# The last batch's output product as seven block products for eight, with the block sums on GpSimd and VectorE

## The chip, the cores and the metric

One core of one Trainium2 chip. The metric is the device time of one execution in microseconds (us). A time is the median of several executions. Times were taken in rounds against the kernel before on the same chip; all runs quoted are in the normal ("fast") state of the chip.

## The reference

Two attentions, then a small two-layer network. B = 8 batches, H = 8 heads, S = 576 positions, D = 64; the network has 512 inputs, 2048 hidden units and 512 outputs.

```python
def _attn_ref(q, k, v, p):
    scale = 1.0 / np.sqrt(q.shape[-1])
    # sm_attn(q, k, v) = softmax(scale * q k^T) v
    p_packed = sm_attn(p, k, v)          # 32 rows per head
    return sm_attn(q, p_packed, p_packed)

def _moe_ref(x, w_in, w_out):            # x: (4608, 512), heads side by side
    h = x @ w_in
    g = h * np.cos(h)
    return g @ w_out
```

## The kernel before

TensorE is the busy engine. Batch by batch, `h_mm` makes the hidden units of a batch in 16 pieces of 128 (TensorE into PSUM, ScalarE a sine, VectorE the product `gT`), and the output product of the *previous* batch is spread between these as filler matmuls. The last batch has no successor, so its output product stands alone at the end.

Each batch has 576 rows: four chunks of 128, and 64 left over. Two batches' leftovers make one "joint" chunk, copied together by GpSimd.

```python
    def h_mm(b, fc):
        ...
        def rest():
            V.tensor_tensor(out=gT[b][:, fc, :]..., in0=ps[:, :, 0:HS], in1=csv, op=ALU.mult)
            if fc % 8 == 7:
                j0 = (b % 2) * 64
                G.tensor_copy(out=joint[b // 2][:, fc - 7:fc + 1, j0:j0 + 64],
                              in_=gT[b][:, fc - 7:fc + 1, 512:576])
        return rest
    ...
    def tail_chunk(b, c):                       # the joint chunk of the last pair of batches
        osb = o_pool.tile([128, DM], FP32, name="osb")
        for i in range(2):
            cols = slice(i * 256, i * 256 + 256)
            ps = O.tile([128, 256], FP32, name="ot", tag="ot")
            for fc in range(NFC):
                nc.tensor.matmul(ps, joint[b // 2][:, fc, :], w_out_bf[:, fc, cols], ...)
            copy((ACT, V)[i], osb[:, cols], ps)
            for (a, z, rows), q in zip(pieces_of(b, c), (nc.sync, nc.scalar)):
                q.dma_start(out=rows[:, cols], in_=osb[a:z, cols])
    ...
    # the end of the kernel
    out_eng[:] = V, ACT
    set_filler(B - 1)      # drains batch 6, then chunks 0 to 3 of batch 7: 64 matmuls of 512 columns
    fill(1000)
    tail_chunk(B - 1, 4)   # 32 matmuls of 256 columns
```

PSUM is split into a pool `A` of three double banks (for `h_mm` and all else) and a pool `O` of two single banks (output chunks).

## Time and profile before

| | |
|---|---|
| median time | 248.45 us (3 runs), 248.26 with one more |
| span of the profiled execution | 246.8 us |
| TensorE busy | 94% |
| last stretch, from the seven leftover filler matmuls on (223.84) to the last copy's end (243.33) | 19.49 us |
| from there to the end of the span ("store tail") | 3.42 us |

The views give a span to 0.1 us; the ends of spans, and so the store tails, are taken here and below from the trace files, in ns (this span is 246.753 us). The prediction's 3.47 us for the tail comes from the rounded 246.8.

The prediction below shows the lines. They are read like this: a line of the time order has the start in us, the length in us, the engine, the source line, what was written from what, shapes, and a count; in brackets the engine's idle time before it and what ended that. The chain of waits lists, in order of time, what each piece of the path to the end consisted of.

### The profile page before, as it was taken

What the parts mean: (1) busy time and instruction counts of PE and PEld (TensorE: products, weight loads), DVE (VectorE), ACT (ScalarE), POOL (GpSimd) and SP (SyncE); (2) the same over time, 40 slices, a digit from 0 to 9 for tenths busy, and PEclk for the clock granted to TensorE, in tenths of its full rate; (3) what the DMA queues carried; (4) which work ended last, traced back from release to release, by engine and by line L of the source; (5) the groups of instructions that cost most, each with busy time, mean ns of one, the idle gap of its engine ahead of it and who ended that gap; (6) DMA issues with size and microseconds to landing.
All of it is one profiled execution on the core that took longest, in us unless ns stands there. A gap on an engine that the chain in (4) does not pass through costs nothing.

```text
span 246.8 us, 5023 instructions
## 1 busy us (share of the span) xinstructions
PE 233.2 (94%) x1996; PEld 130.9 (53%) x2029; DVE 165.2 (67%) x248; ACT 169.0 (68%) x282; POOL 57.7 (23%) x70
## 2 busy tenths in 40 slices
PE   8788799999999999999999999999999999999993
PEld 3454374566545654565446554565456554665452
DVE  3549987677658776678767766678766684886110
ACT  2369799877576787888787776888778684873000
POOL 8342533240400355004503105030500100001000
PEclk9999999999999999999999999999999999999999
DMA  6999999999899999999999997999571113111133
GB/s 90 202 203 206 205 206 228 194 241 151 179 202 184 192 175 214 218 198 142 222 211 187 172 201 91 198 166 171 109 154 27 45 43 84 43 31 57 47 84 85
DMA packets 64231, 37.36 MB, mean 151 GB/s; under 512 B 36848, under 2 KB 59632, under 8 KB 64208
## 3 DMA queue, kind: packets, MB, share of 16 engines
q0 software_dynamic: 23152, 18.75, 50.0%
q1 hardware_dynamic: 40624, 18.09, 35.1%
q8 instruction: 16, 0.26, 0.4%
q10 hardware_dynamic: 432, 0.20, 0.4%
q14 instruction: 7, 0.06, 0.1%
HBM read 37.22 MB, written 9.44 MB: 189 GB/s over the span
## 4 chain that ended last, share of the span: by engine, by line
PE 78%; DMA 12%; issue 2%; DVE 2%; ACT 2%; POOL 2%; DVEq 0%; POOLq 0%
PE ot L309 46%; PE psA L256 21%; DMA vbf<-in_v_dram 10%; PE psA L207 3%; DMA a1T<-a 2%; PE psA L129 2%; PE psA L183 2%; DVE gT L263 2%; PE ot L295 1%; PE psA L233 1%; ACT cosT L260 1%; POOL vp L77 1%; ACT ppT L75 1%; POOL kbf L84 1%; PE ot L104 0%
## 5 line engine op out<-in xcount | busy, mean ns | idle before, releaser
L309 PE MATMUL ot<-w_out_bf,gT 128*128 128x512 bf16 x482 | 127.5, 379 | 2.0 <-issue 1.1
L263 DVE TENSOR_TENSOR gT<-psA,cosT 128x576 bf16<-128x576 f32 x128 | 93.8, 755 | 28.9 <-ACT cosT L260 28.2
L260 ACT ACTIVATE cosT<-psA 128x576 bf16<-128x576 f32 x128 | 82.4, 652 | 24.6 <-PE psA L256 22.1
L256 PE MATMUL psA<-a2n,PPW 128*128 128x288 bf16 x512 | 83.8, 286 | 1.6 <-DVE gT L263 0.4
L309 PEld LDWEIGHTS <-gT 128*128 128x128 bf16 x512 | 47.8, 98 | 43.4 <-issue 6.7
L256 PEld LDWEIGHTS <-PPW 128*128 128x128 bf16 x512 | 49.3, 98 | 34.6 <-issue 3.9
L77 DVE CAST PPW<-psA 128x1024 bf16<-128x1024 f32 (+1 forms) x23 | 26.9, 1175 | 11.6 <-PE psA L207 11.5
L267 POOL COPY joint<-gT 128x512 bf16<-128x512 bf16 x16 | 9.9, 616 | 82.5 <-DVE gT L263 82.5
L77 DVE COPY osb<-ot 128x512 f32<-128x512 f32 (+1 forms) x22 | 14.9, 678 | 17.5 <-PE ot L309 7.7
L77 POOL COPY vp<-vbf 96x3072 bf16<-96x3072 bf16 x7 | 19.3, 2751 | 6.3 <-DMA vbf<-in_v_dram 6.3
L75 ACT COPY osb<-ot 128x512 f32<-128x512 f32 (+1 forms) x15 | 8.5, 567 | 15.3 <-PE ot L309 10.6
L243 DVE SCALAR_TENSOR_TENSOR a2n<-a2u,r,lns 128x576 bf16<-128x576 bf16 x16 | 12.3, 812 | 7.3 <-ACT lns L241 7.3
L235 ACT ACTIVATE lns<-psA 128x576 f32<-128x576 f32 x16 | 10.1, 650 | 7.1 <-PE psA L233 6.5
L140 ACT ACTIVATE a<-psA 128x576 bf16<-128x576 f32 x16 | 10.3, 647 | 6.7 <-PE psA L129 6.7
L309 PE MATMUL ot<-w_out_bf,joint 128*128 128x512 bf16 x47 | 12.8, 379 | 0.1
L225 ACT ACTIVATE a2u<-psA,rs 128x576 bf16<-128x576 f32 x16 | 11.0, 737 | 1.4 <-PE psA L129 1.3
L75 ACT CAST ppT<-psA 64x128 bf16<-64x128 f32 x24 | 6.2, 260 | 7.0 <-DVE ppT L77 5.9
L207 PE MATMUL psA<-w_in_bf,ppT 64*32 64x512 bf16 x224 | 10.1, 380 | 0.0
L241 ACT ACTIVATE lns<-lns 128x576 f32<-128x576 f32 x16 | 10.0, 676 | 0.0
L347 PE MATMUL ot<-wz 128*128 128x512 bf16 x23 | 7.7, 468 | 1.4 <-DVE wz L358 1.2
L527 POOL COPY gate<-kT 1x1 bf16<-1x1 bf16 x3 | 0.5, 181 | 32.3 <-DMA kT<-kbf 32.3
L183 PEld LDWEIGHTS <-vp 96*128 96x128 bf16 x192 | 6.5, 98 | 2.3 <-issue 1.2
(73 smaller groups left out, 152.7 us busy)
## 6 DMA issues: line engine op xcount, KB each, us to landing
kbf<-in_k_dram POOLq DMA_DIRECT2D x8, 576.0 KB, 12.6
vbf<-in_v_dram POOLq DMA_DIRECT2D x8, 576.0 KB, 7.6
qbf<-in_q_dram POOLq DMA_DIRECT2D x8, 576.0 KB, 10.1
out_dram<-osb SPq DMA_DIRECT2D x24, 192.0 KB, 2.7
out_dram<-osb SPq DMA_DIRECT2D x22, 128.0 KB, 2.4
w_in_bf<-in_moe_w_in_dram POOLq DMA_DIRECT2D x4, 512.0 KB, 17.3
w_out_bf<-in_moe_w_out_dram POOLq DMA_DIRECT2D x4, 512.0 KB, 21.2
out_dram<-osb SPq DMA_DIRECT2D x26, 64.0 KB, 2.1
```

The costliest lines, as they stand in the source:

```text
L75: ACT.copy(out=out, in_=in_)
L77: eng.tensor_copy(out=out, in_=in_)
L140: ACT.activation(out=a1[b % 2][:, y, :, 0:TP].rearrange("p (e m) x -> p e m x", e=2), in_=ps[y][:, :, 0:HS].rearrange("p e (m x) -> p e m ...
L183: nc.tensor.matmul(ps[:, hp * 64:(hp + 1) * 64], vp[b][:, c, hp * 128:(hp + 1) * 128], a1T[b][0:TP, :, j, 32 * hp:32 * hp + 32], start=(j ...
L207: nc.tensor.matmul(ps[y][32 * x:32 * x + 32, :], ppT[b % 2][r, 2 * x + y, :], w_in_bf[r, x, n * 512:(n + 1) * 512], start=True, stop=True)
L225: ACT.activation(out=a2u[b][:, y].rearrange("p (e x) -> p e x", e=2), in_=ps[y][:, :, 0:HS], func=AF.Exp, scale=rs1[b][:, y:y + 1])
L235: ACT.activation(out=lns[b][:, y].rearrange("p (e x) -> p e x", e=2), in_=ps[:, :, 0:HS], func=AF.Ln)
L243: V.scalar_tensor_tensor(out=a2n[b][:, y], in0=a2u[b][:, y], scalar=r1[b][:, y:y + 1], in1=lns[b][:, y], op0=ALU.mult, op1=ALU.mult)
L256: nc.tensor.matmul(ps[:, e, 0:HS], PPW[b][:, y, fc * 128:(fc + 1) * 128], a2n[b][:, y, e * HS:(e + 1) * HS], start=(y == 0), stop=(y == 1))
L260: ACT.activation(out=csv, in_=ps[:, :, 0:HS], func=AF.Sin, bias=PI_HALF)
L263: V.tensor_tensor(out=gT[b][:, fc, :].rearrange("p (e x) -> p e x", e=2), in0=ps[:, :, 0:HS], in1=csv, op=ALU.mult)
L309: nc.tensor.matmul(pss[c], w, w_out_bf[:, fc, :], start=(fc == 0), stop=(fc == NFC - 1))
```

## The change

The intent: in the last batch the output product of each pair of chunks (256 rows) is a 2 x 2 block product. Winograd's form of Strassen's algorithm makes it from seven block products, not eight, at the price of sums of blocks. Sums of weight blocks (`T`) go to GpSimd during batch 6, behind a one-element copy that waits for batch 6's normalised probabilities (the gate). Sums of activation blocks (`S`) go half to GpSimd, as the first eight pieces of batch 7 become ready, half to VectorE at the end. The joint chunk moves to the second place, as 16 matmuls of 512 columns. VectorE adds the products up as they leave PSUM.

```diff
+    def T_sums():
+        G.tensor_copy(out=gate, in_=a2n[B - 2][0:1, 1, 0:1])
+        ...
+        for out, in0, in1 in ((T[0], B_blk(0, 1), B_blk(0, 0)), (T[1], B_blk(1, 1), T[0]),
+                              (T[2], B_blk(1, 1), B_blk(0, 1)), (T[3], B_blk(1, 0), T[1])):
+            G.tensor_tensor(out=out, in0=in0, in1=in1, op=ALU.subtract)
+
+    def S_sums(b, p, eng, k0, k1):
+        ...
+        for out, in0, in1, op in ((S1, A21, A22, ALU.add), (S2, S1, A11, ALU.subtract),
+                                  (S3, A11, A21, ALU.subtract), (S4, A12, S2, ALU.subtract)):
+            eng.tensor_tensor(out=out, in0=in0, in1=in1, op=op)
+
+    def last_out(b):
+        ... # o1, o2, u: where the sums of products gather; store: the output DMAs
+            m = {1: (A_blk(b, 2 * p, 0, 0, 8), B_blk(0, 0)), 2: (A_blk(b, 2 * p, 1, 0, 8), B_blk(1, 0)),
+                 3: (S4, B_blk(1, 1)), 4: (A_blk(b, 2 * p + 1, 1, 0, 8), T[3]),
+                 5: (S1, T[0]), 6: (S2, T[1]), 7: (S3, T[2])}
+            def then4(ps, p=p, o1=o1, o2=o2, u=u):
+                plus(o2, ps, u[:, 1])
+                store(o2, 2 * p + 1)
+                plus(o1[:, 2], ps[:, 1], o1[:, 2])
+            def then3(ps, p=p, o1=o1):
+                plus(o1[:, 1], ps, o1[:, 2])
+                store(o1, 2 * p, 1, (nc.sync, nc.scalar, nc.sync))
+        ...
+        def products(names):
+            ps = O.tile([128, 2, 256], FP32, name="ot", tag="ot")
+            for i, (p, n) in enumerate(names):
+                lhs, rhs = pr[p][0][n]
+                for kp in range(8):
+                    nc.tensor.matmul(ps[:, i], lhs[:, kp, :], rhs[:, kp, :], start=kp == 0, stop=kp == 7)
+            ... # then the addition of each
+        products(((0, 1),))
+        ... # the joint chunk: 16 matmuls of 512 columns, ACT.copy, store
+        for names in (((0, 2), (0, 6)), ((0, 7),), ((0, 4), (0, 5)), ((0, 3), (1, 1)),
+                      ((1, 2), (1, 6)), ((1, 7),), ((1, 4), (1, 5)), ((1, 3),)):
+            products(names)
@@ slot: after pieces 3 and 7 of batch 7, GpSimd's share of the S sums
+            if s == B - 1 and fc in (3, 7):
+                for p in range(2):
+                    S_sums(s, p, G, fc // 2 - 1, fc // 2 + 1)
@@ the end
-    out_eng[:] = V, ACT
-    set_filler(B - 1)
     fill(1000)
-    tail_chunk(B - 1, 4)
+    for p in range(2):
+        S_sums(B - 1, p, V, 4, 8)
+    last_out(B - 1)
```

(Cut: tile allocations, the renaming of S to SQ, helper functions.)

> **What bounds the kernel now.** I read the page's busy shares and slices first, then the chain of waits, then the time order of the last 25 us engine by engine, and last the groups of instructions of that stretch. The page and the end of the chain:
>
> ```profile
> PE 233.2 (94%) x1996; PEld 130.9 (53%) x2029; DVE 165.2 (67%) x248; ACT 169.0 (68%) x282; POOL 57.7 (23%) x70
> ...
> PE   8788799999999999999999999999999999999993
> DVE  3549987677658776678767766678766684886110
> POOL 8342533240400355004503105030500100001000
> ...
> 224.00 4.32 PE ot L309 x20
> 228.32 0.05 issue
> 228.37 10.74 PE ot L309 x49
> 239.11 0.05 issue
> 239.16 3.67 PE ot L295 x32
> ```
>
> The reader is to see a TensorE busy to the end, with every other engine nearly idle in the last four slices (24.7 us). The chain's last 19 us are TensorE alone: the output product of the last batch. Whatever shortens that stretch shortens the kernel, unless another engine comes onto the path. The time order of that stretch:
>
> ```profile
> 223.84 15.27 PE L309 MATMUL ot<-w_out_bf,gT 128*128 128x512 bf16 x69
> 239.16 3.66 PE L295 MATMUL ot<-w_out_bf,joint 128*128 128x256 bf16 x32
> ...
> 224.02 1.47 DVE L263 TENSOR_TENSOR gT<-psA,cosT 128x576 bf16<-128x576 f32 x2 [0.16 <-ACT cosT L260]
> 225.55 0.69 DVE L77 COPY osb<-ot 128x512 f32<-128x512 f32 x1
> ...
> 225.55 0.62 POOL L267 COPY joint<-gT 128x512 bf16<-128x512 bf16 x1 [6.76 <-DVE gT L263]
> ...
> 242.91 0.42 DVE L77 COPY osb<-ot 128x256 f32<-128x256 f32 x1 [2.85 <-PE ot L295]
> ```
>
> The 69 matmuls are seven left over from batch 6 and 64 of batch 7 (two records must be missing). One 512-column matmul follows another after 0.2155 us (eight take 1.89 us from 200.34, of which the last stands for 0.38: 1.51/7). So batch 7 starts at 223.84 + 7 x 0.2155 = 225.35, and 64 x 0.2155 later it is 239.14, which is where the joint chunk starts. That chunk's 256-column matmuls follow each other after (3.66 - 0.27)/31 = 0.1093 us. The last product is therefore 13.79 + 3.50 = 17.29 us of TensorE time. After it come 0.25 us to the last copy, 0.42 us of copy to 243.33, and 3.47 us to the end at 246.8 for the store and its landing.
>
> **What the Trainium skill says.**
> (1) "TensorE: Matmul & The Clock Gate", Back-to-back issue gap: N/2.4 + 2.5 ns when warm, 109 ns for 256 columns and 216 for 512. This trace agrees (109.3 and 215.5). The same section also gives about 131 ns sustained at 512 columns; the trace does not show that.
> (2) "GPSIMD Engine Reference", section 3.1: a two-input operation takes about 2.6 cycles per element and 4497 ns for 2048 fp32 elements. The kernel before has no such instruction on GpSimd; its copies with one input go at about 0.9 ns per element (2.75 us for 3072), so bf16 isn't shown for two inputs.
> (3) "VectorE: DVE Perf Modes", the perf-mode tier table: a bf16 tensor_tensor in SBUF runs at two elements per cycle, 1224 ns for 2048, and one with a PSUM operand at one. The trace agrees on the second: 757 ns for 576 elements against 692 for a 512 copy.
> (4) "SBUF — State Buffer", Who interferes with whom: a VectorE instruction with two SBUF inputs and a GpSimd instruction that reads SBUF exclude each other for the whole instruction; with at most one SBUF input and no two-port mode there is no contention. The trace agrees with the second half: a product gT beside a GpSimd copy keeps its 0.76 us.
>
> ```profile
> 192.07 0.62 POOL L267 COPY joint<-gT 128x512 bf16<-128x512 bf16 x1 [14.85 <-DVE gT L263]
> ...
> 192.39 0.76 DVE L263 TENSOR_TENSOR gT<-psA,cosT 128x576 bf16<-128x576 f32 x1 [0.38 <-ACT cosT L260]
> ```
>
> The first half is not shown, since no instruction with two SBUF inputs meets GpSimd work.
>
> **The change part by part.**
>
> *TensorE.* Removed: the 64 matmuls of 512 columns and 32 of 256. Added: two chunk pairs x 7 products x 8 matmuls of 256 columns = 112, and the joint chunk as 16 matmuls of 512 columns. 112 x 0.1093 = 12.24; 16 x 0.2155 = 3.45; sum 15.69 us. Saved: 17.29 - 15.69 = 1.60 us. Two things eat into the full eighth: a 256-column matmul costs 1.4% more than half of a 512 one, and the joint chunk saves nothing but that.
>
> *Weight sums.* Four GpSimd operations of 2048 elements, each about 4.5 us by (2): 18 us. They stand after a gate on the normalised probabilities of batch 6, ready at 182.70 in the time order of VectorE, so they run to about 201. Everything VectorE does meanwhile reads at most one SBUF tensor, so nothing is slowed by (4). The next two-SBUF-input work on VectorE is the normalisation of batch 7 at 209.25: 8 us to spare. Cost on the path: 0.
>
> *Sums of the last activations.* On GpSimd 16 operations of 256 elements, eight after the fourth activation chunk (about 215.1) and eight after the eighth (218.1). Each takes 256 x 2.17 = 0.56 us plus about 0.1 fixed (a one-element copy takes 0.18), and one in four waits for its predecessor. I take eight as 5.6 us: 215.1 to 220.7, a joint copy of 0.62, then 221.3 to 226.9, and the second joint copy to 227.5. On VectorE eight of 512 elements, 157 + 512/1.92 = 424 ns each by (3), from 225.5 to about 229. TensorE runs the first product from 225.35 to 226.22 and the joint chunk to 229.67, so the first sum it needs from VectorE is due at about 231.0: no wait.
>
> *The joint chunk's second half* needs the GpSimd copy at 226.22 + 8 x 0.2155 = 227.95. The copy is ready at 227.5 if nobody stands in the way. But from 225.5 VectorE's sums compete with GpSimd's last two or three sums and that copy. If they alternate, the copy is delayed by one or two VectorE operations, to 228.4. I put the wait at 0.5 us.
>
> *VectorE at the end.* Products leave PSUM by additions: 424 ns for 256 columns, 0.69 us for 512. There are two output banks, and twice a single product of 0.87 us has to cover the hand-over of 0.25 + 0.69 + 0.1 = 1.04 us: two waits of 0.17 us. Then the last: TensorE's last product would end 1.60 - 0.33 = 1.27 us earlier, but VectorE has two additions (0.69 + 0.42) from the pair in front, issued 0.25 us after that pair's end; they take until 0.24 us after the last product is ready. So the last addition ends about 1.27 - 0.24 = 1.03 us earlier than 243.33, at 242.3.
>
> *Store.* Same size as before (128 rows of 1 KB, on two queues), but 256 KB of the chunk in front were issued 0.85 us earlier and may still move: 0.1 us.
>
> Sum: 1.60 - 0.33 - 0.24 - 0.1 - 0.5 = 0.43 us faster; 248.45 - 0.43 is about 248.0. The wait for the joint copy can hardly be negative and can be large, so I move to **248.1 us**.
>
> **The rivals.**
> 1. *GpSimd is fast enough.* If bf16 sums take 0.4 us each, GpSimd is done at 224.5 and the copy at about 226.6. Then the wait falls away: 0.9 us faster, 247.5. For it: bf16 is half the bytes of the page's fp32 case. Against it: GpSimd's one-input copies in bf16 already run at about one element per cycle, so bytes don't look like its limit.
> 2. *The joint copy becomes the bound.* If VectorE's eight sums run through before GpSimd gets the port again, the copy ends at about 229 + three sums + 0.62 = 231.6: a wait of 3.6 us, and the change loses about 2.7 us, 251.2. If they alternate but the sums take 0.75 us, the wait is about 2 us and the change loses 1.1, 249.6. For it: the copy stands last in GpSimd's strict order and has 0.45 us of slack by my sum. Against it: the port passes when an instruction ends, and VectorE's second and sixth sums wait for their predecessor, which leaves GpSimd a gap.
> 3. *The weight sums last longer than 26 us* (over 6.6 us each). Then they block the normalisation of batch 7, with TensorE having only 13 filler matmuls (2.8 us) to cover it: up to 4 us lost. For it: nothing in the trace; against it: the page's 4.5.
> 4. *Weight loads bind the 256-column stream.* There are 128 loads for 96 before; a load lasts 98 ns, under the 109 of a matmul, and the 32 of the tail show that they hide. Unlikely.
>
> **Range and chances.** The gain is bounded by 1.60 us (0.6%), so faster by over 2% (5 us) is out: 0.01. A loss of 5 us needs rivals 2 and 3 together or an effect that I don't see: 0.04. Within 2%: 0.95. Rival 1 gives the low side, 247.0 with a little for the spread between runs (0.6 us over three); rival 2 in its milder form gives the high side, 249.9.
>
> **What would show each step right or wrong.** In the changed profile: the 112 product matmuls following each other after 0.109 us and the last one about 1.3 us earlier, less the joint wait (right step for TensorE); the weight sums on GpSimd between 182.7 and 202, and the normalisation of batch 7 still about 0.81 us per operation (right on the gate); the GpSimd activation sums at 0.65 us and the second joint copy ending near 228 with TensorE idle about 0.5 us in the middle of the joint chunk; the two additions in front of the last one running back to back. Wrong: TensorE idle over 1.5 us before the joint chunk's ninth matmul or before the products with sums, VectorE's sums stretched far beyond 0.42 us, gT products above 0.8 us in batch 6, or an unchanged end with the store landing later.

## The result, and the profile after

The changed kernel takes 246.92 us (median of 4 runs), the kernel before 248.26 (4 runs). The ratio is 0.9944, 95% interval 0.9927 to 0.9961. A ratio is the mean time of one kernel's fast runs over that of the other's of the same rounds, so it isn't quite the ratio of the medians. Within 2%, but the gain is about 1.4 us where I had 0.35, and the time is just under the range's low end of 247.0. The output passes the check for correctness; what the bf16 sums cost in accuracy isn't on record.

The page's busy shares and slices of the changed kernel:

```profile
PE 235.1 (96%) x2061; PEld 134.2 (55%) x2061; DVE 171.0 (70%) x262; ACT 169.4 (69%) x283; POOL 84.7 (35%) x91
...
PE   8888799999999999999999999999999999999993
DVE  2449987677667877678857666678667865788542
POOL 8252543241310454005411305020529960099000
```

GpSimd (POOL) now works in batch 6 and just before the end, and VectorE works through the last slices. TensorE stays busy to the end. The end of the chain of waits (L360 are the products, L370 the joint chunk, L328 VectorE's additions):

```profile
223.86 1.51 PE ot L387 x7
225.37 0.87 PE ot L360 x8
226.24 3.45 PE ot L370 x16
229.70 8.87 PE ot L360 x80
238.57 0.01 issue
238.57 1.92 PE ot L360 x16
240.50 0.02 issue
240.52 0.69 DVE osb L328
241.21 0.34 DVE o L328
...
241.64 0.42 DVE o L328
```

The joint chunk runs its 16 matmuls in 3.45 us = 16 x 0.2155, without a gap: the wait that I feared isn't there. The last three pieces are VectorE's additions of the last pair, one after another, as the prediction had it. Why there was no wait shows in GpSimd's and VectorE's time order (L303 weight sums, L314 activation sums, L267 the joint copy):

```profile
195.01 4.06 POOL L303 TENSOR_TENSOR T<-w_out_bf,T 128x2048 bf16<-128x2048 bf16 x1
...
224.82 0.67 POOL L314 TENSOR_TENSOR S<-gT 128x256 bf16<-128x256 bf16 x1
225.44 0.88 POOL L314 TENSOR_TENSOR S<-gT,S 128x256 bf16<-128x256 bf16 x1
226.27 0.80 POOL L267 COPY joint<-gT 128x512 bf16<-128x512 bf16 x1
```

```profile
225.37 0.42 DVE L314 TENSOR_TENSOR S<-gT 128x512 bf16<-128x512 bf16 x1
225.83 0.78 DVE L314 TENSOR_TENSOR S<-S,gT 128x512 bf16<-128x512 bf16 x1
226.53 0.82 DVE L314 TENSOR_TENSOR S<-gT 128x512 bf16<-128x512 bf16 x1
227.28 0.41 DVE L314 TENSOR_TENSOR S<-gT,S 128x512 bf16<-128x512 bf16 x1
```

The two engines do meet. VectorE's first sum goes first; GpSimd's sum, started 0.07 us later, takes 0.88 us where its neighbours take 0.67. VectorE's second sum then ends 0.29 us after GpSimd's end (226.61 against 226.32), and its third 0.28 us after the copy's (227.35 against 227.07): one alone takes 0.41 to 0.42 us, so each waits out what is left of GpSimd's instruction. They alternate. But only one sum and the copy of GpSimd's were left by then, so the copy was delayed by only 0.4 us and ended at 227.07; TensorE needed it at about 227.80, 0.73 us later (eight matmuls of 0.2155 after the joint chunk's first at 226.08).

The steps side by side, from the profiles. "Stretch" counts from the start of the seven leftover fillers, so that the start of the stretch, which moves by some tenths between executions, drops out.

| | before | changed | difference |
|---|---|---|---|
| stretch to TensorE's end | 18.98 | 17.67 | -1.31 |
| TensorE's end to VectorE's last end | 0.51 | 0.71 | +0.20 |
| VectorE's last end to the span's end | 3.42 | 3.19 | -0.23 |
| sum | 22.91 | 21.57 | -1.34 |

(The start of the stretch was 223.84 and 223.69.) The first two are the predicted 1.27 and 0.24. Two things differ from the prediction: no wait for the joint copy, and a shorter store tail.

### The profile page after: what moved, and what is told of

Its sections match the earlier page's. It is cut to its first block, busy times and chain, and to the rows that moved or that the text cites. A ratio compares the mean times of both kernels' runs of the same rounds, so it can differ in the third digit from the quotient of the medians.

```text
span 245.3 us, 5164 instructions
## 1 busy us (share of the span) xinstructions
PE 235.1 (96%) x2061; PEld 134.2 (55%) x2061; DVE 171.0 (70%) x262; ACT 169.4 (69%) x283; POOL 84.7 (35%) x91
## 4 chain that ended last, share of the span: by engine, by line
PE 80%; DMA 11%; DVE 3%; ACT 3%; issue 1%; POOL 1%; DVEq 0%; POOLq 0%
PE ot L387 43%; PE psA L256 22%; DMA w_in_bf<-in_moe_w_in_dram 7%; PE ot L360 5%; DMA vbf<-in_v_dram 3%; PE psA L207 3%; DVE gT L263 2%; PE psA L129 2%; ACT cosT L260 2%; PE psA L183 2%; PE psA L233 1%; PE ot L370 1%; ACT ppT L75 1%; DVE vp L77 0%; PE psA L166 0%
## 5 line engine op out<-in xcount | busy, mean ns | idle before, releaser
L387 PE MATMUL ot<-w_out_bf,gT 128*128 128x512 bf16 x448 | 119.3, 380 | 0.0
L387 PEld LDWEIGHTS <-gT 128*128 128x128 bf16 x448 | 41.6, 98 | 35.7 <-issue 6.5
L267 POOL COPY joint<-gT 128x512 bf16<-128x512 bf16 x16 | 10.0, 627 | 38.3 <-DVE gT L263 38.3
L77 DVE COPY osb<-ot 128x512 f32<-128x512 f32 x18 | 12.4, 691 | 2.1 <-PE ot L387 1.4
L425 PE MATMUL ot<-wz 128*128 128x512 bf16 x25 | 8.9, 496 | 1.2 <-DVE wz L436 1.2
L314 POOL TENSOR_TENSOR S<-gT 128x256 bf16<-128x256 bf16 x8 | 5.4, 671 | 12.5 <-DVE gT L263 12.5
L84 POOL DMA_DIRECT2D vbf<-in_v_dram x8 | 6.2, 775 | 6.4 <-DVE vp L77 4.4
```

The costliest lines, as they stand in the source:

```text
L77: eng.tensor_copy(out=out, in_=in_)
L387: nc.tensor.matmul(pss[c], w, w_out_bf[:, fc, :], start=(fc == 0), stop=(fc == NFC - 1))
```

## The experiments

Theory A: the predicted sum is right but for a wait that doesn't exist, because GpSimd has slack. The rivals: the block sums still cost something, the new order of the chunks gives part of the gain, or the copy is nowhere near the path. All numbers called "stretch" or "tail" below are read from the runs' traces as in the table above. Three runs (before_again, x_half, x_tail) found no chip and gave no result; they were repeated unchanged as before_ctl, half_pair and tail_rows.

### The control: both kernels again

a_again and after_ctl are the changed kernel, before_ctl the kernel before, unedited.

> The changed kernel once more, as the control of these runs. Theory A (the wait for the joint chunk's copy that I had put at 0.5 us is not there, and the rest is TensorE's 1.60 us less the bank waits and VectorE's tail): 1.1 to 1.4 us faster than the kernel before. Theory B (part of the 1.4 us came from elsewhere, such as an earlier start of the last batches or a shorter store): the profile shows the last addition again about 1.1 us earlier but the store tail (last addition to the end) and the start of batch 7 differ from the first profile by 0.1 to 0.2 us, and the ratio settles nearer 1.1 us.

> The kernel before once more, as a control of the method and of the store tail. In its first profile 3.47 us lie between the last addition or copy and the end; in nine profiles of kernels whose joint chunk isn't last it was 3.14 to 3.23. Theory A (the joint chunk's stores, two of 64 rows, land later than ones of 32 and 96 rows): again 3.4 to 3.5 us. Rival (the first profile was a late landing by chance): 3.1 to 3.3 us. The ratio to the kernel before should be 1 within 0.1%.

> The changed kernel, on the same chip as the two versions below, to compare with. About 1.4 us faster than the kernel before.

| run | time (us) | ratio, 95% interval | stretch to VectorE's last end | tail |
|---|---|---|---|---|
| a_again | 247.06 | 0.9938 (0.9923 to 0.9954) | 18.37 | 3.17 |
| after_ctl | 246.89 | 0.9936 (0.9921 to 0.9950) | 18.38 | 3.15 |
| before_ctl | 248.49 | 1.0005 (0.9991 to 1.0019) | 19.50 | 3.41 |

The stretch repeats to 0.02 us: about 1.12 us of the gain are work on the engines. The tail of the kernel before is again long, 3.41, so it wasn't chance; the changed kernel's is 3.15 to 3.19. The tail gives the other 0.22 to 0.27 us.

### Do the sums cost anything? x_nosums

```diff
-slot(... + [(6, T_sums)] * (s == B - 2) + ...)    # no weight sums
-S_sums(...)                                       # no activation sums, on either engine
-3: (S4, B_blk(1, 1)), 4: (..., T[3]), 5: (S1, T[0]), 6: (S2, T[1]), 7: (S3, T[2])
+3: (A12, B22), 4: (A22, B21), 5: (A21, B12), 6: (A11, B22), 7: (A22, B12)    # wrong on purpose
```

> Wrong result on purpose: all sums of weights and of activations are left out, and the products take plain blocks instead; products, additions and stores stay. Theory A (the sums and their contention are all off the path): the same time as a_again within 0.15 us, TensorE's order and gaps unchanged in the last batch. Rival (the sums, or GpSimd's and VectorE's meeting, cost some of the gain): 0.3 us or more faster than a_again.

247.06 us, ratio 0.9943 (0.9926 to 0.9960), the same as a_again's 247.06 in the same rounds; the stretch is 18.37 in both. The result is wrong, as meant (relative error 0.33). So 20 GpSimd and 8 VectorE operations, and their meeting at the end, cost no time where they stand. The 0.5 us that I had entered for the meeting is 0.

### How much slack has the joint copy? x_late2, x_late4

Two, or four, more sums of 256 elements on GpSimd ahead of the last joint copy, into a tile that nobody reads.

```diff
+            if b == B - 1 and fc == 15:
+                for _ in range(2):          # 4 in x_late4
+                    G.tensor_tensor(out=spare, in0=A_blk(b, 0, 0, 0, 2), in1=A_blk(b, 1, 0, 0, 2), op=ALU.add)
```

> Two more sums of 256 elements on GpSimd ahead of the last joint copy. Theory A (0.9 us of slack in the changed kernel): the copy ends at about 228.4 to 228.8 in the changed kernel's time, TensorE waits 0.4 to 0.8 us, and the kernel is that much slower. Rival (no such slack, the copy already sets TensorE's pace): slower by the whole 1.3 to 1.7 us. Rival (copy far from the path): no change.

> Four more sums of 256 elements on GpSimd, into a tile that nobody reads, ahead of the last joint copy. From the changed kernel's profile the copy ended at 227.07 and TensorE needs it at about 227.96, so 0.9 us of slack; four sums at 0.63 to 0.85 us each put the copy at 229.6 to 230.5. Theory A: TensorE waits 1.7 to 2.5 us in the middle of the joint chunk and the kernel is that much slower than a_again. Rival (the copy is far from the path): under 0.5 us slower.

x_late2: 247.88 us, ratio 0.9984 (0.9972 to 0.9997). x_late4: 249.70 us, ratio 1.0064 (1.0036 to 1.0093). TensorE's and GpSimd's time order in x_late2:

```profile
225.96 1.89 PE L374 MATMUL ot<-w_out_bf,joint 128*128 128x512 bf16 x8
228.63 1.90 PE L374 MATMUL ot<-w_out_bf,joint 128*128 128x512 bf16 x8 [0.78 <-POOL joint L271]
...
226.17 1.65 POOL L268 TENSOR_TENSOR spare<-gT 128x256 bf16<-128x256 bf16 x2
227.77 0.80 POOL L271 COPY joint<-gT 128x512 bf16<-128x512 bf16 x1
```

The copy ends at 228.57 and the ninth joint matmul starts 0.06 us later, 0.95 us after its turn (225.96 + 8 x 0.2155 = 227.68). The two sums put the copy 1.62 us later than in the changed kernel (whose 227.07 is 226.95 on this run's clock, which runs 0.12 us ahead). So the slack was 1.62 - 0.95 = 0.67 us, and beyond it the wait counts in full: the stretch to VectorE's end is 19.33, 0.95 above 18.38. (I had expected a wait of 0.4 to 0.8 us, from a slack of 0.9.) The mechanism of the prediction was right: a copy that is late enough does stop TensorE. Its slack was wrong by 1.1 us: minus 0.45, a copy at 228.4 needed at 227.95.

x_late4 waits 2.40 us, but its stretch is 22.62, so 4.24 us longer. After the gap TensorE runs slower for a while, as its time order in x_late4 shows:

```profile
230.27 2.60 PE L374 MATMUL ot<-w_out_bf,joint 128*128 128x512 bf16 x8 [2.40 <-POOL joint L271]
232.67 1.91 PE L364 MATMUL ot<-w_out_bf,gT 128*128 128x256 bf16 x8
```

The eight products in the second line follow each other after 0.21 us, twice the usual 0.109; the granted clock was 0.50 from 232.7 to 234.6. The profiled execution took 251.18 us, one of the two slowest of six (clock 0.991 over the span in both); the others took 249.4 to 249.8 at a clock of 0.997 to 1.0, 2.4 to 2.8 us above a_again, at and above the upper end of the 1.7 to 2.5 that I expected. The wait alone would make 247.06 + 2.40 = 249.46, so these four probably had no half clock; they have no profile.

### What is the gate worth? x_nogate

```diff
 def T_sums():
-    G.tensor_copy(out=gate, in_=a2n[B - 2][0:1, 1, 0:1])
```

> The changed kernel without the gate: GpSimd starts the weight sums after its permute of batch 7's values, about 177.2, instead of 182.8. Theory A (a GpSimd sum and a VectorE instruction with two SBUF inputs exclude each other for the whole instruction): the normalisation of batch 6 at about 181 meets 4.06 us sums; its two operations take up to 4 us longer, TensorE idles 1.5 to 4 us in front of batch 6, and the kernel is 1 to 4 us slower than the changed one. Rival (the two share the port and slow each other a little): under 0.5 us slower.

256.79 us, ratio 1.0350 (1.0322 to 1.0377): 9.9 us slower than the changed kernel, over twice what I expected. The profiled execution was the slowest of four (258.16 us). The time order of GpSimd, VectorE and TensorE at batch 6:

```profile
177.43 4.07 POOL L302 TENSOR_TENSOR T<-w_out_bf 128x2048 bf16<-128x2048 bf16 x1
...
185.59 4.56 POOL L302 TENSOR_TENSOR T<-w_out_bf 128x2048 bf16<-128x2048 bf16 x1
...
178.98 2.55 DVE L152 TENSOR_SCALAR rs<-r 128x2 f32<-128x2 f32 x1
...
182.04 8.72 DVE L243 SCALAR_TENSOR_TENSOR a2n<-a2u,r,lns 128x576 bf16<-128x576 bf16 x2
...
186.30 0.47 PE L256 MATMUL psA<-a2n,PPW 128*128 128x288 bf16 x2 [3.38 <-DVE a2n L243]
190.81 0.64 PE L256 MATMUL psA<-a2n,PPW 128*128 128x288 bf16 x2 [4.05 <-DVE a2n L243]
...
192.10 1.16 PE L256 MATMUL psA<-a2n,PPW 128*128 128x288 bf16 x4
```

The two normalisations take 8.72 us together, against 1.55 in the changed kernel: each waits out one 4 us weight sum. Even a two-element tensor_scalar in front of them waits 2.4 us of its 2.55. TensorE idles 7.4 us, and runs its next products at half pace (four matmuls of 288 columns 1.16 us, usually 0.65; the granted clock was 0.50 from 190.8 to 195.0). I had expected up to 4 us for the two operations together; each was blocked for most of a weight sum, and the clock came on top. So the gate is not a detail of the change; the sums pay off only because of where they stand.

### Does the new order alone help? x_order, tail_rows, last_one

x_order keeps eight products, but puts the joint chunk second, as 16 matmuls of 512 columns, and cuts the last plain chunk into two halves of columns, stored as the joint chunk's were. tail_rows is the kernel before with the joint chunk's stores cut differently. last_one is x_order with chunk 1, whose rows split 64 and 64, at the end in place of chunk 3 (96 and 32).

```diff
-        set_filler(B - 1)                                        # x_order, against the kernel before
         fill(1000)                                               # stays: it drains batch 6
-        tail_chunk(B - 1, 4)
+        for c, eng in ((0, ACT), (4, V), (1, ACT), (2, V)):      # last_one: 0, 4, 3, 2
+            one(c, eng)
+        # then chunk 3 (last_one: chunk 1) in two halves of 256 columns, stored on two queues

-            q.dma_start(out=rows[:, cols], in_=osb[a:z, cols])   # tail_rows: 64 rows on each queue
+            nc.sync.dma_start(...)      # rows 0 to 32
+            nc.scalar.dma_start(...)    # rows 32 to 64
+            nc.scalar.dma_start(...)    # rows 64 to 128
```

> Eight products as in the kernel before, but with the joint chunk moved to the second place as 16 matmuls of 512 columns, and the last plain chunk cut into two halves of columns. Theory A (the gain is the seven products alone): within 0.15 us of the kernel before, since TensorE has 68 x 0.2155 ... in all 64 matmuls of 512 and 32 of 256 still, 17.3 us. Rival (moving the joint chunk off the end, away from the last copies, gives part of the gain): 0.3 us or more faster than the kernel before.

> The kernel before, with the joint chunk's halves stored as 32 rows on one queue and 32 and 64 on the other, in place of 64 and 64. Theory A (the split of the rows makes the late landing): 3.15 to 3.25 us from the last copy to the end, and 0.2 us faster than the kernel before. Rival (it is something else of the joint chunk's place, or chance): as before_ctl, no faster.

> As x_order, eight products, but chunk 1 comes last in place of chunk 3; its rows split 64 and 64 as the joint chunk's do, without being the joint chunk. Theory A (stores of 64 and 64 rows land later than of 96 and 32): 3.35 to 3.5 us from the last copy to the end, as in the kernel before. Rival (it is the joint chunk's place in the output): 3.1 to 3.25 us, as x_order.

| run | last store's rows | time (us) | ratio, 95% interval | stretch to last end | tail |
|---|---|---|---|---|---|
| before, before_ctl | 64 + 64 | 248.26, 248.49 | | 19.50 | 3.42, 3.41 |
| x_order | 96 + 32 | 248.24 | 0.9985 (0.9966 to 1.0003) | 19.50 | 3.14 |
| last_one | 64 + 64 | 248.39 | 1.0003 (0.9983 to 1.0024) | 19.50 | 3.42 |
| tail_rows | 32 + 32 + 64 | 248.42 | 1.0002 (0.9987 to 1.0018) | 19.50 | 3.37 |

The order alone doesn't move the stretch, so the 1.1 us come from the seven products. For the tail, last_one against x_order speaks for the split of the rows: the same position in the kernel, another split, and the long tail is back. tail_rows doesn't decide: the third piece's issue waited for the second's on the same queue (0.37 us), so the split came with a later start. Part of it can be seen in the instructions that issue the last two stores. For 64 rows each takes 0.47 to 0.51 us (before, before_ctl, last_one), in x_order 0.32 for 96 rows and 0.38 for 32; the last one ends 0.54 us after VectorE's last end there, 0.41 in x_order and 0.42 in the changed kernel. So about 0.12 of the 0.22 to 0.27 us lie in the issue; the rest comes after it (2.88 us to the end of the span against 2.73 to 2.77), and no run explains it. The differences of the times, 0.1 to 0.2 us, are inside their intervals; only the profiles' tails separate, so I call the split likely and not shown.

### Is the saving in proportion? half_pair, half_banks

Only the first pair of chunks by seven products, the second pair plain; half_banks also takes the products' banks from the idle pool A.

```diff
-((0, 3), (1, 1)), ((1, 2), (1, 6)), ((1, 7),), ((1, 4), (1, 5)), ((1, 3),)
+((0, 3),)     # then chunk 2 plain, and chunk 3 in two halves of columns
```

> Only the first pair of chunks by seven products; the second pair as plain chunks, the last cut into two halves of columns as in x_order. Theory A (each pair saves TensorE 8 x 8 - 7 x 8 matmuls of 256 columns, 0.78 us here, less one bank wait of 0.13 us): from the end of batch 7's activations to TensorE's end 18.2 to 18.35 us, between the 18.99 of x_order and the 17.67 of the changed kernel, and 0.5 to 0.8 us faster than x_order. Rival (a fixed cost of the products that only two pairs repay): no faster than x_order.

> As half_pair, with the products in the idle PSUM pool's banks. Theory A (half_pair lost 0.54 us of its 0.79 to two waits for a bank): from the last fillers' start to TensorE's end 18.20 us within 0.05, the plain value of 18.99 less 64 - 56 matmuls of 256 columns and the 1.4% that they cost over halves of 512; 0.5 us faster than half_pair. Rival (the products have a fixed cost): above 18.4 us.

half_pair: 247.97 us, ratio 0.9982 (0.9965 to 0.9999), stretch to TensorE's end 18.74: only 0.25 us saved against x_order's 18.99, below what I expected. Most of the loss is a wait for a bank: the plain chunk, 0.87 us behind a single product, needs the bank whose contents VectorE is still adding. That chunk in TensorE's time order of half_pair:

```profile
235.80 3.63 PE L379 MATMUL ot<-w_out_bf,gT 128*128 128x512 bf16 x15 [0.24 <-DVE o L328]
```

One of its 16 matmuls has no record. It starts 0.41 us after its turn (234.52 + 8 x 0.1093 = 235.39); a second wait, 0.14 us, lies before the pair of products in front. half_banks: 18.19, 0.80 below x_order and within 0.01 of the value expected from counting matmuls. So the products have no fixed cost on TensorE: each pair saves 0.79 us if banks are free. Its time was 247.02, ratio 0.9942 (0.9924 to 0.9960), 0.95 us below half_pair where I expected 0.5, which is better than its stretch says; its stretch started 0.4 us earlier than the kernel before's and its tail was 3.01, so I don't read that total as the products' doing.

### A better version: x_banks, x_best, best_ctl, best_swap

x_banks takes the products' PSUM from pool A, idle by then. x_best also computes the last pair's fifth product alone, ahead of the fourth, so that VectorE's additions of the fifth run beside the fourth. best_swap does the second pair of chunks first.

```diff
-            ps = O.tile([128, 2, 256], FP32, name="ot", tag="ot")
+            ps = psa()[:, 0, :].rearrange("p (a x) -> p a x", a=2)
-                      ((1, 2), (1, 6)), ((1, 7),), ((1, 4), (1, 5)), ((1, 3),)):
+                      ((1, 2), (1, 6)), ((1, 7),), ((1, 5),), ((1, 4),), ((1, 3),)):      # x_best
+    # after product 5: o2's second half and o1's sum; after product 4: o2's first half, then the store
```

> The products take the three double banks of the other PSUM pool, which is idle by then, in place of the pool with two banks. Theory A (the 0.29 us between the products in the changed profile are waits for VectorE to empty a bank): they vanish, TensorE's last product ends 0.29 us earlier and the kernel is 0.2 to 0.35 us faster than the changed one. Rival (they are issue or weight-load gaps): no change.

> As x_banks, and in the last pair the fifth product comes alone before the fourth, so that VectorE's two additions of the fifth run beside the fourth product, and one of 0.42 us is left in front of the last. Theory A (VectorE's two additions in front of the last one hold it up by 0.2 us): 0.15 to 0.25 us faster than x_banks, 0.35 to 0.6 us faster than the changed kernel, about 246.4. Rival (the end is set by the stores' landing and not by the last addition): no faster than x_banks.

> x_best again, beside the changed kernel. Its chain from the last fillers to the last addition was 17.81 us against 18.37, so 0.4 to 0.6 us faster than after_ctl if the chain decides; x_best's own time, on another chip, was 0.2 to 0.4 us better.

> x_best with the second pair of chunks first, so that the last store is chunk 0's, 96 rows on the first queue and 32 on the second, in place of 32 and 96. If the split decides the tail, 3.0 to 3.15 us in place of 3.2, and 0.1 us faster than best_ctl; if not, the same.

| run | time (us) | ratio, 95% interval | stretch to TensorE's end | from there to VectorE's last end | tail |
|---|---|---|---|---|---|
| after_ctl (the changed kernel) | 246.89 | 0.9936 (0.9921 to 0.9950) | 17.66 | 0.72 | 3.15 |
| x_banks | 246.79 | 0.9937 (0.9924 to 0.9949) | 17.36 | 0.71 | 3.17 |
| x_best | 246.55 | 0.9931 (0.9917 to 0.9944) | 17.35 | 0.46 | 3.16 |
| best_ctl (x_best again) | 246.35 | 0.9914 (0.9898 to 0.9929) | 17.35 | 0.46 | 3.15 |
| best_swap | 246.84 | 0.9942 (0.9922 to 0.9963) | 17.36 | 0.46 | 3.59 |

x_banks removes 0.31 us of waits between products, and 17.36 is what counting gives: 7 x 0.2155 + 16 x 0.2155 + 112 x 0.1093 = 17.20, and 0.16 for the end of the last. Its time, on another chip than the changed kernel, doesn't show the gain. x_best takes another 0.25 us off the end. The last two additions in VectorE's time order of x_best:

```profile
240.29 0.42 DVE L328 TENSOR_TENSOR osb<-psA,u 128x256 f32<-128x256 f32 x1
241.17 0.42 DVE L328 TENSOR_TENSOR o<-psA,o 128x256 f32<-128x256 f32 x1 [0.45 <-PE psA L370]
```

VectorE is idle 0.45 us before the last addition, so it no longer holds it up. On one chip with the changed kernel (best_ctl and after_ctl) it is 0.54 us faster, against 0.56 by the stretches, and each of its six times is below each of the other's. So this version beats both kernels. best_swap was meant to shorten the tail by the split 96 + 32; it is slower than best_ctl by 0.5 us with the same stretch. Its profile fell on its slowest execution (248.21 us, the stretch starting 1.3 us late), but why its tail is long can be read there. The stores on SyncE's queue (SPq) in the time orders of best_swap and of best_ctl:

```profile
241.96 1.11 SPq L323 DMA_DIRECT2D out_dram<-osb  x2
243.17 0.53 SPq L323 DMA_DIRECT2D out_dram<-o  x1
```

```profile
240.63 0.79 SPq L323 DMA_DIRECT2D out_dram<-osb  x2
241.50 0.38 SPq L323 DMA_DIRECT2D out_dram<-o  x1
```

The swap also put a chunk with 64 and 64 rows in front of the last store, on the same queue. Its two stores take 1.11 us to issue, best_ctl's 0.79. So the last store, whose data VectorE had ready at 242.81, starts its issue at 243.17 (in best_ctl 0.03 us after VectorE's end) and takes longer. The last issue ends 0.89 us after VectorE's end against 0.41, and from there it is 2.70 us to the end against 2.74: the late issue is the whole of the longer tail. So best_swap is no test of the last store's split alone, and the split stays likely. Its other executions (246.71 to 247.04) have the same order of stores and probably lose their 0.5 us in the same way; they have no profile.

## Why the prediction was right or wrong

- *TensorE saves 1.60 us, less 0.33 of bank waits:* right. The profile has 1.31 for 1.27; x_banks shows the bank waits as 0.31.
- *VectorE holds the end up by 0.24 us:* right, 0.20; x_best removes 0.25.
- *Weight sums, 4.5 us each, off the path:* right, at 4.06 us; they ended at 199.1, 10 us before batch 7's normalisation. That a GpSimd sum and a VectorE instruction with two SBUF inputs exclude each other, which I took from the skill alone, x_nogate shows.
- *The joint copy, a wait of 0.5 us:* wrong, and the main step that failed. Each term of that sum was a little too long. The first eight activation sums took 5.24 us and the last eight 5.25 without the meeting, where I had 5.6 each; GpSimd's meeting with VectorE cost 0.4 us and I had 0.9, since one sum and the copy were left at that point and not two or three. Together the copy was 1.2 us earlier than in my sum, which turned a wait of 0.5 into 0.67 us of slack (x_late2, x_nosums).
- *The store, 0.1 us later:* wrong in sign. The tail is 0.23 us shorter (0.22 to 0.27 over the controls). I had compared sizes and not what the last stores were; the kernel before ends in two stores of 64 rows, and in all three profiles that end so (before, before_ctl, last_one) the tail is 3.41 to 3.42 us. About 0.12 us of it lie in longer issues; that the split of the rows makes the rest is likely and not shown. No rival had a shorter tail in it.
- *The move from 248.0 to 248.1* put the asymmetric risk of rival 2 on top of a wait that was itself too long. Rival 1 was the nearest: GpSimd was fast enough, though by sums of 0.63 us and not by 0.4.

By terms: 1.31 - 0.20 + 0.23 = 1.34 us against the predicted 1.27 - 0.24 - 0.1 - 0.5 = 0.43.

## What to carry to other kernels

A queue whose last item another engine waits for should be summed in its measured durations, and where it comes within a microsecond of the need, the slack itself is worth a run: add work until the end moves. A block product by fewer multiplications pays on a matmul-bound end if its sums stand where they hold nothing up; here the same weight sums, started 5.4 us earlier (177.43 for 182.83), cost 9.9 us. Look for banks that have become idle before accepting waits for banks.

## What the Trainium skill lacked or had wrong

- "GPSIMD Engine Reference", section 3.1, has two-input sums in fp32 only (4497 ns for 2048). In bf16 the runs show 4.06 us for 2048 elements and 0.67 us for 256, following each other after 0.63 us, or 0.74 where one waits for its predecessor.
- "SBUF — State Buffer", Who interferes with whom, is confirmed (0.42 us sums became 0.78 and 0.82), but it doesn't say how two busy queues take turns: they alternate, one instruction each, so a GpSimd sum of 4 us costs each VectorE instruction that needs the port up to 4 us (8.72 us for two of 0.81). That a tensor_scalar can contend too, as the page says, shows here even at two elements (2.55 us for 0.17).
- "TensorE: Matmul & The Clock Gate", Part 1, puts the return to the half clock after an idle window of about 3.4 us. In x_late4's profile an idle gap of 2.40 us was followed by matmuls at half pace (granted clock 0.50), in x_late2's one of 0.78 us was not. The 131 ns for sustained matmuls of 512 columns, in the page's section Back-to-back issue gap, was not seen; it was 215.5 ns at full clock.
- No page that I read has it that the split of the rows of a last store bears on its landing: 3.41 to 3.42 us with 64 and 64 rows, 3.00 to 3.19 with 32 and 96, but for best_swap, whose last store was issued late (3.59). Issuing a last store took 0.47 to 0.51 us for 64 rows and 0.31 to 0.39 for 32 or 96, once 0.53 (best_swap).
